# A fused attention and gated-convolution kernel: another order of its hand-written instruction list

## The chip, the core and the metric

The kernel runs on one core of a Trainium2 chip. A core has TensorE (matrix products, written PE in the profile, its weight loads PEld), VectorE (DVE), ScalarE (ACT), GpSimd (POOL) and SyncE (SP), which each work through a list of their own in order and wait for one another by semaphores, and 16 DMA engines that all lists share. The metric is device time in microseconds (us). Four runs of the kernel before took 222.66 to 223.70 us, median 223.43.

## What is computed

Eight batches of 576 positions, eight heads of 64. First linear attention with cosine-weighted features, then a gate with a circular convolution and an output product:

```
r   = max(x, 0);  phi(x) = [r * cos_w, r * sin_w]        # q and k
kv  = phi(k)^T v;  z = sum of phi(k);  x = phi(q) kv / (phi(q) z + 1e-6)
x1, x2, x3 = split(x @ w_proj)
x2_conv = irfft(rfft(x2) * rfft(filter))                 # over the 576 positions
out = (x1 * x2_conv * x3) @ w_out
```

## The kernel before

The work is cut into steps, each a Python generator: one `next` on it issues a few instructions and stops. A plan, a string written into the kernel (lines 905 to 987), names the steps in the order in which their pieces are issued, 1139 pieces in all; `run` (line 890) reads it. As every engine works through what it was given in the order of the plan, this string is the order of all five lists. A word is a step with its indices, the first of them the batch; `*3` takes three pieces; after an apostrophe stands the engine where there is a choice (`'v` VectorE; for `pk` and `pq`, `'a` ScalarE). Without it an eviction goes to ScalarE (`ev`, line 131), a `pk` or `pq` piece to VectorE. A leading `~` makes a load wait (`hold`, line 148) for the last VectorE instruction and the last DMA transpose before it in the plan.

Per batch b the steps are:

- loads `Lq`, `Lk`, `Lv` (line 167, issued by GpSimd, converting to 16 bit; six buffers `raw`, so those of batch b-2 are overwritten); for batch 0's first half `Sk`, `Sv` (SyncE). `Lw`, `Lf`, `Lo` load weights and the filter. `pad` clears the unused rows of a buffer.
- `pk` (line 505, ten pieces), `pq` (519, six pieces, the first over 2560 columns, the others over 512), `va` (539): features of k and q, and v, made on ScalarE or VectorE.
- `kv` (556), `qt` (573: transposes of q's features, on TensorE for batches 0 and 1, by DMA later), `num` (600: product, then three VectorE pieces that divide and write `att`).
- `fx` (629) and `xp` or `xt` (666, 659): `att` into the order that the transform wants, and transposed.
- `pr` (676), `dft` (701), `mul` (718, four VectorE pieces), `inv` (765): the projection of x2 and its convolution in frequency space.
- `ga`, `gb` (730): the two gate projections; `g` (751) their product; `y` (786, six VectorE pieces); `out` (837: product, eviction, store); `end` (863): the last batch's output tile by tile.
- Set-up tables made from index patterns: `io` (GpSimd), `cols`, `rows`, `tf`, `ti`, `th`, `h`, `feo`; `warm` is twelve products on zeros at the start.

Every TensorE step takes one of four PSUM units (line 70), which is free again when its eviction is done; output tiles go through three buffers `os` (846, 872) and one small one (854). So the place of an eviction in ScalarE's or VectorE's list says when TensorE may go on. Steps of several batches are interleaved: while one batch is in its gates, the next is in its attention.

Of the kernel before, what the change touches and what calls it, by code (L numbers as in the profile page):

```python
# [17 lines left out]
def kernel(  # L18
# [48 lines left out]
    late = {}  # L67
# [822 lines left out]
    def run(plan, **batch):  # L890
# [12 lines left out]
    manual = tc.manual_schedule()  # L903
    manual.__enter__()
    run("""
        cols io0 pad1 Sk0.0 pad2 cols io2 rows io1 cols rows th tf warm0.12 cols*5 Sv0.0
        rows pad0 th'v rows*3 th'v cols*3 rows pk0.0'a*2 rows pk0.0'a*2 tf pk0.0 rows
        pk0.0'a tf pk0.0 cols*2 rows va0.1 cols ones0 rows*2 pk0.0*2 rows va0.0'v pk0.0'a
        th'v Lq0.0 Lq0.1 kv0.0 rows pq0.0 pq0.0'a*4 pq0.0 pq0.1*2 qt0.1 pq0.1*3 Lk0.1 qt0.0
        pq0.1'a qt0.2 kv0.0 qt0.1'b num0.1 tf pk0.1'a pk0.1*3 tf pk0.1 qt0.0'c num0.0 pk0.1  # L910
        ones1 pk0.1'a pk0.1*2 Lv0.1 va0.2 num0.0 num0.1 pk0.1'a va0.3'v qt0.2'b Lw0 kv0.1*2
        num0.1 num0.0 num0.1 cols Lw2 num0.0 qt0.3 rows Lq1.2 num0.2*2 cols*2 xp0.0 qt0.3'b
        rows num0.2 rows num0.2 Lk1.2 xp0.0*2 xp0.0'a num0.3*4 xp0.1 Lv1.2 ga0.0 gb0.3 Lw1
        xp0.1*2 pad4 cols pad5 ti xp0.1'v cols pad3 Lf gb0.0*2 tf ga0.0 gb0.0 ga0.0 Lf
        gb0.3*2 ga0.3 gb0.2 ti tf th ~Lq2.2 cols ~Lk2.2 cols pq1.2*2 pq1.2'a pq1.2*2 pq1.2'a
        rows gb0.2 ga0.3 ga0.1*2 ga0.3'v ti cols fx0.1 fx0.0 pk1.2 gb0.2 pk1.2 gb0.1*2 ga0.1
        fx0.3 fx0.1 pk1.2*2 fx0.0'v ga0.2 pk1.2 fx0.2 th gb0.1 fx0.3 fx0.2 ga0.2*2 pk1.2
        tf'v pk1.2*4 qt1.0 va1.0'v kv1.2 va1.1'v kv1.2 th kv1.2 qt1.1 g0.0.2 qt1.0'v th
        ~Lq3.1 tf qt1.0'v qt1.1'v qt1.2 qt1.1'v qt1.2 ~Lk3.0 qt1.2 num1.0*3 tf pr0.1 th
        num1.1 num1.0 num1.2 g0.2.2 num1.1 tf ~Lq3.0 num1.2 num1.1 pr0.1 tf ti pr0.0 num1.2  # L920
        num1.1 qt1.3 num1.2 pr0.0 pr0.2 qt1.3 dft0.0 feo0 pr0.2 dft0.0 feo1 h0 qt1.3'v xp1.0
        ti xp1.0 pq2.2 fx1.1 pq2.2 h0'v h1 ~Lv2.2 pq2.2 xp1.0 pq2.2 pk2.2 xp1.0'v pk2.2
        pk2.2'a h0 fx1.1 pk2.2 num1.3*3 pq2.2 num1.3 pq2.2 qt2.3 h2 qt2.0 fx1.2 h1 pk2.2 h1
        pk2.2 xp1.1 fx1.3 xp1.1 ~Lk3.1 ~Lq4.1 ~Lv3.1 h2 fx1.2 xp1.1'v fx1.3 xp1.1'v fx1.0
        pk2.2*2 dft0.1 dft0.1'v ~Lo dft0.2 ga1.0 fx1.0 dft0.2 mul0 ti mul0 pr1.0 pr1.2 ti*2
        mul0 ga1.0 mul0 pr1.1 pr1.1'v pr1.0 ga1.0 inv0.1 inv0.0 ~Lq4.0 ti pk2.2 late pr1.2
        dft1.2 dft1.0 dft1.2'v inv0.1 dft1.1 pk2.2 inv0.0 inv0.2 va2.0'v dft1.0 kv2.2 pq3.2
        va2.1'v inv0.3 kv2.2 y0.0.2 ~Lk4.1 y0.0.2 dft1.1 inv0.2 ga1.2*2 mul1 gb1.2 mul1
        qt2.1 kv2.2 num2.0 ~Lv3.0 qt2.2 num2.0 inv0.3 num2.1 pq3.2'a ga1.2 gb1.2 ~Lv4.0
        num2.1 num2.0 num2.1 num2.0 num2.1 gb1.3*2 mul1*2 gb1.2 gb1.1*2 pq3.2'a pq3.2 gb1.3  # L930
        pq3.2'a ga1.1 pk3.2 gb1.1 num2.2 ~Lk4.0 num2.2*3 y0.0.2 ga1.1 y0.0.2 fx2.1 y0.2.2
        ga1.1 y0.2.2 gb1.0*2 pk3.2'a fx2.1 inv1.1 fx2.2 pk3.2 gb1.0 inv1.1 fx2.2 ga1.3
        y0.2.2 ga1.3 inv1.0 inv1.0'v ga1.3 xp2.0 num2.3*3 xp2.0*3 num2.3 pk3.2 inv1.3*2
        y0.0.2 inv1.2*2 fx2.0*2 fx2.3*2 g1.0.2 ga2.0 xp2.1*2 pr2.0 xp2.1*2 pq3.2 ga2.0
        y0.2.2 qt3.0 va3.0'v y1.0.2 pk3.2 pk3.2'a*2 pk3.2 y0.2.2 pk3.2'a pq4.2 pr2.1 ga2.0
        qt3.2 pq4.2 out0.0 pr2.2 pr2.1 pr2.0 out0.0 dft2.1 y1.0.2 dft2.0 ~Lq5.0 va3.1'v
        y1.0.2 ~Lq5.1 ~Lv4.1 y1.0.2 pk3.2 ~Lv5.0 qt3.1 y1.2.2*2 pr2.2'v dft2.1 y1.2.2 dft2.2
        kv3.2*2 y1.0.2 gb2.1 y0.2.2 gb2.1 dft2.0 g1.2.2 y0.0.2 pq4.2'a ~Lv5.1 qt3.3 dft2.2'v
        kv3.2 gb2.0*2 mul2*2 num3.0*4 ~Lk5.0 gb2.1 gb2.0 gb2.3 pk4.2'a gb2.3*2 ~Lk5.1 out0.2
        ga2.2*2 fx3.0 out0.2 pq4.2'a ga2.1 mul2*2 ga2.2 fx3.0 num3.1*2 num3.2*2 pk4.2'a  # L940
        ga2.1 num3.1 pk4.2 out0.1 num3.2 num3.1 y1.2.2 ga2.1 num3.2 num3.3*2 pk4.2 pk4.2'a
        num3.3*2 ga2.3 gb2.2 ga2.3 xt3 pq4.2'a gb2.2 out0.1 fx3.1 fx3.2 ga2.3 inv2.1 gb2.2
        fx3.3 pq4.2 qt4.0 qt4.1 pk4.2'a pk4.2*2 fx3.3 fx3.1'v fx3.2'v inv2.1 pk4.2'a inv2.0
        pk4.2 inv2.0 g2.2.2 qt4.2 va4.0'v va4.1'v y2.0.2*2 pr3.0*2 pr3.1 pq5.2 pr3.1 kv4.2
        g2.0.2 y1.2.2 ~Lk6.0 ~Lq6.0 kv4.2*2 pq5.2'a pr3.2 ga3.0 pk5.2 pr3.2'v pk5.2 y1.2.2
        ga3.0 inv2.2 out0.2 dft3.2 ~Lk6.1 inv2.2'v dft3.0*2 dft3.2'v dft3.1*2 num4.0 inv2.3
        pk5.2*2 inv2.3 num4.0 y1.0.2 pq5.2'a gb3.1 num4.1 num4.0*2 num4.2 mul3 gb3.1 num4.1
        ~Lq6.1 pq5.2'a out1.0*2 num4.2 num4.1 pq5.2'a qt4.3 num4.1 ga3.1*2 pq5.2'a y2.0.2
        num4.2 gb3.0 num4.2 y2.0.2 y2.2.2 num4.3 gb3.0 num4.3 out0.0 out1.1*2 y2.2.2 num4.3
        gb3.3 fx4.0 qt5.2 num4.3 fx4.2 gb3.2 mul3 xt4 gb3.3'v ga3.2 qt5.1 mul3 pk5.2 fx4.0  # L950
        fx4.2 mul3 fx4.1 g3.0.2 inv3.0 qt5.0 gb3.2 qt5.3 fx4.3 y2.2.2 ga3.2 fx4.1 pk5.2*3
        inv3.0'v fx4.3 pk5.2 inv3.1 inv3.1'v y2.2.2 y3.0.2*2 pk5.2'a pr4.0 y3.0.2 inv3.3
        pr4.0 y2.2.2 inv3.3 out1.2*2 pr4.2 out1.2 pr4.1 y3.0.2 ~Lq7.0 va5.0'v kv5.2 y2.0.2
        va5.1'v pr4.1'v inv3.2 pq6.2 pr4.2 kv5.2 ga4.0 pk6.2*2 ~Lv6.1 ga4.0'v inv3.2 kv5.2
        out0.1 dft4.2 pq6.2 pq6.2'a*2 pq6.2 dft4.1 dft4.0 ga3.3 dft4.2 dft4.0'v pk6.2 dft4.1
        mul4 ~Lq7.1 num5.0*3 ga3.3 ~Lv6.0 num5.0 ~Lk7.1 gb4.1 num5.1*2 g3.2.2 pk6.2'a*2
        out2.0 gb4.1 y3.2.2 out1.0 out2.0 pk6.2'a pk6.2 pk6.2'a gb4.0 num5.1 gb4.0 num5.1
        out2.1 mul4 num5.2 ~Lk7.0 ga4.1 ga4.2 out2.1 fx5.1 num5.2 y2.2.2 num5.2*2 num5.3*4
        ga4.1 ga4.2 fx5.0 fx5.1 fx5.2 fx5.0 y2.0.2 gb4.2 gb4.2'v mul4 fx5.3 fx5.2 out2.2
        fx5.3 va6.0 pq6.2'a g4.0.2 pr5.2 pr5.2'v pk6.2'a pr5.0*2 out2.2 y3.2.2*2 pr5.1 mul4  # L960
        pk6.2'a va6.1'v pr5.1'v inv4.1*2 y3.2.2 inv4.0 inv4.3 dft5.1 xt5 inv4.0 inv4.3 qt6.0
        dft5.2 pq7.2 dft5.0 ga5.0 dft5.1 dft5.2'v pq7.2*2 y3.2.2 y4.0.2 y3.2.2 dft5.0 out1.1
# [24 lines left out]
    """)
    manual.__exit__(None, None, None)

# [29 lines left out]
```

## Time and profile before

| | |
|---|---|
| median of 4 runs | 223.43 us (222.66 to 223.70) |
| profiled execution: its time, its span | 223.55 us, 221.7 us |
| gate products (line 736), TensorE | 512 matmuls, 71.2 us, mean 286 ns |
| projection of x2 (680) | 160 matmuls, 34.6 us, mean 381 ns |
| output product (824) | 128 matmuls, 30.1 us, mean 379 ns |
| `att` products (116), VectorE | 32, 26.0 us, mean 820 ns |
| evictions of 576 columns: ScalarE, VectorE | about 0.64 us, about 0.75 us |
| HBM read, written | 33.69 MB, 9.44 MB; 194 GB/s over the span |

The profiled execution is one of the runs. Durations in it overlap: an instruction is counted from its start to its end, and the next one on the same engine often starts some 0.1 us earlier than that end. In a group's line stand the source line, engine, operation, result and operands, the count, the busy time, the mean in ns, and the idle time ahead of it with what ended it. In the chain of waits the columns are start, duration and what ran. The view by stretch gives busy time and number of instructions for TensorE, its weight loads, VectorE, ScalarE and GpSimd, then the clock granted to TensorE, the DMA share and GB/s. Lines 111, 116 and 138 are helpers that many steps use, so names of results tell the step.

### The profile page before, as it was taken

Reading aid. Unit: us, or ns where it says so; the run is one execution under the profiler, and the core shown is the slowest. Engines: PE = TensorE matmul, PEld = TensorE weight load, DVE = VectorE, ACT = ScalarE, POOL = GpSimd, SP = SyncE. Lnnn points to the kernel's source line nnn. Section 1 sums busy time; section 2 is a strip of 40 time slices with the busy share of each in tenths; the row PEclk is TensorE's granted clock in tenths of the full one; section 3 lists DMA queues with packets and bytes.
Section 4 is the critical chain, followed back from the end, with each engine's and each line's share of the span. In section 5 each row is a group of like instructions: output and inputs, shape, how many; then the busy total and the mean of one; then the engine's idle time right before and its main releaser. Section 6 shows DMA issues by size and latency. Waiting matters only on the chain.

```text
span 221.7 us, 5869 instructions
## 1 busy us (share of the span) xinstructions
PE 207.8 (94%) x2316; PEld 143.5 (65%) x2316; DVE 195.0 (88%) x473; ACT 170.8 (77%) x275; POOL 63.5 (29%) x105
## 2 busy tenths in 40 slices
PE   7398989999999999999999999999999999999990
PEld 2286777574788567766685768576876667477630
DVE  7898999999999989998999997999988897689930
ACT  4795998998988999878876787977887736476651
POOL 8892425221963077202700184002200000000000
PEclk9859999999999999999999999999999999999999
DMA  5999999999999999999999999997999950823084
GB/s 174 180 188 192 192 209 192 181 116 198 152 177 189 173 168 183 167 204 153 186 163 229 208 185 182 201 250 154 110 188 141 327 134 9 199 95 135 19 260 166
DMA packets 90907, 38.39 MB, mean 173 GB/s; under 512 B 58944, under 2 KB 86592, under 8 KB 90880
## 3 DMA queue, kind: packets, MB, share of 16 engines
q0 software_dynamic: 38944, 16.26, 60.5%
q1 hardware_dynamic: 51568, 21.17, 45.6%
q10 hardware_dynamic: 368, 0.59, 0.7%
q8 instruction: 18, 0.29, 0.5%
q14 instruction: 9, 0.07, 0.1%
HBM read 33.69 MB, written 9.44 MB: 194 GB/s over the span
## 4 chain that ended last, share of the span: by engine, by line
PE 71%; DVE 14%; DMA 5%; ACT 3%; issue 2%; POOL 2%; ACTq 0%; DVEq 0%; POOLq 0%
PE x L736 22%; PE x L680 13%; PE out L824 10%; PE dft L711 4%; PE kv L563 4%; PE num L606 4%; PE fx L634 3%; PE inv L770 3%; PE inv L774 3%; DMA out_dram<-os 3%; DMA raw<-in_q_dram 3%; DVE kp L111 2%; DVE yf L116 2%; DVE qp L111 2%; PE fx L640 1%
## 5 line engine op out<-in xcount | busy, mean ns | idle before, releaser
L736 PE MATMUL x<-xt,wp 128*128 128x288 f16 x512 | 71.2, 286 | 0.3 <-ACT xt L138 0.2
L736 PEld LDWEIGHTS <-wp 128*128 128x128 f16 x512 | 47.9, 98 | 15.4 <-issue 3.2
L680 PE MATMUL x<-wp,fx 128*128 128x512 f16 (+1 forms) x160 | 34.6, 381 | 0.0
L824 PE MATMUL out<-wo,y 128*128 128x512 f16 x128 | 30.1, 379 | 0.0
L138 ACT ACTIVATE os<-out 128x1024 f32<-128x1024 f32 (+2 forms) x24 | 18.3, 767 | 12.0 <-PE out L824 11.8
L116 DVE TENSOR_TENSOR att<-num,rcp 128x640 f16<-128x640 f32 x32 | 26.0, 820 | 0.6
L680 PEld LDWEIGHTS <-fx 128*128 128x128 f16 (+1 forms) x160 | 13.6, 100 | 15.0 <-issue 2.1
L138 ACT CAST x0s<-x 128x576 f16<-128x576 f32 x27 | 17.3, 643 | 6.1 <-PE x L736 5.6
L138 ACT CAST x2s<-x 128x576 f16<-128x576 f32 x28 | 17.8, 639 | 4.8 <-PE x L736 4.7
L138 ACT ACTIVATE x2f<-x 128x1024 f16<-128x1024 f32 (+1 forms) x18 | 16.2, 903 | 6.6 <-PE x L680 5.6
L158 POOL DMA_DIRECT2D raw<-in_q_dram x14 | 11.2, 797 | 32.0 <-ACT xf L138 17.4
L824 PEld LDWEIGHTS <-y 128*128 128x128 f16 x128 | 12.1, 98 | 12.6 <-issue 0.4
L138 ACT CAST fx<-fx 128x576 f16<-128x576 f32 x29 | 17.8, 649 | 2.1 <-PE fx L640 1.8
L138 ACT CAST eq<-inv 128x576 f16<-128x576 f32 x26 | 16.0, 648 | 3.8 <-PE inv L774 3.0
L158 POOL DMA_DIRECT2D raw<-in_k_dram x13 | 10.1, 778 | 27.3 <-DVE ye L116 13.9
L563 PE MATMUL kv<-va,kp 128*128 128x65 f16 x320 | 12.9, 197 | 4.6 <-DVE va L134 4.6
L770 PE MATMUL inv<-itab,yf 128*128 128x144 f16 x128 | 16.9, 226 | 0.2 <-DVE yf L116 0.2
L774 PE MATMUL inv<-itl,yf 128*128 128x288 f16 x64 | 16.8, 286 | 0.0
L158 POOL DMA_DIRECT2D raw<-in_v_dram x13 | 10.5, 806 | 21.7 <-DVE rcp L116 16.9
L563 PEld LDWEIGHTS <-kp 128*128 128x128 f16 x320 | 12.1, 100 | 6.1 <-ACT kp L514 4.0
L606 PEld LDWEIGHTS <-qpt 128*128 128x128 f16 x320 | 13.5, 100 | 3.4 <-issue 0.9
L606 PE MATMUL num<-kvs,qpt 128*128 128x65 f16 x320 | 14.8, 197 | 0.7 <-ACT qpt L138 0.5
(163 smaller groups left out, 431.1 us busy)
## 6 DMA issues: line engine op xcount, KB each, us to landing
out_dram<-os SPq DMA_DIRECT2D x30, 256.0 KB, 3.1
raw<-in_q_dram POOLq DMA_DIRECT2D x12, 256.0 KB, 7.1
raw<-in_k_dram POOLq DMA_DIRECT2D x11, 256.0 KB, 6.6
raw<-in_v_dram POOLq DMA_DIRECT2D x11, 256.0 KB, 6.7
wp<-in_moe_w_proj_dram POOLq DMA_DIRECT2D x3, 512.0 KB, 9.1
raw<-in_q_dram POOLq DMA_DIRECT2D x2, 512.0 KB, 11.8
raw<-in_k_dram POOLq DMA_DIRECT2D x2, 512.0 KB, 13.2
raw<-in_v_dram POOLq DMA_DIRECT2D x2, 512.0 KB, 10.4
```

The source lines that it names most:

```text
L111: last_dve[0] = nc.vector.tensor_scalar(out=out, in0=in0, scalar1=s1, scalar2=s2, op0=op0, **({"op1": op1} if op1 else {}))
L116: last_dve[0] = nc.vector.tensor_tensor(out=out, in0=in0, in1=in1, op=op)
L138: return nc.scalar.copy(out=out, in_=in_) if mul is None else nc.scalar.mul(out=out, in_=in_, mul=mul)
L158: first = queue.dma_start(out=rw[:, to, 0 : 4 * D], in_=src[b, hs, 0:NM].rearrange("h (p j) d -> p h (j d)", j=4),)
L563: nc.tensor.matmul(u[:, g, ds((h % 4) * 65, 65)], kp[:, j, h].rearrange("p a b -> p (a b)"), va[:, h, j, 0:65], start=(j == 0), stop=(j == ...
L606: nc.tensor.matmul(u[:, hh, ds(t * 65, 65)], qpt_buf[:, h, ds(t * 128, 128)], kvs[:, h // 4, ds((h % 4) * 65, 65)], start=True, stop=True,)
L680: nc.tensor.matmul(dst, fx[:, c, ds(128 * ch, n)], wp16[:, c, ds(DM, DM)], start=(c == cs[0]), stop=(c == cs[-1]),)
L711: nc.tensor.matmul(u[ds(32 * x, 32), comp, 0:n], st, mv, start=True, stop=True)
L736: nc.tensor.matmul(u[:, hf, 0:HS], wp16[:, i, ds(w * DM + c * 128, 128)], xt[:, i, ds(HS * hf, HS)], start=(i == 0), stop=(i == NC - 1),)
L770: nc.tensor.matmul(u[:, comp, ds(par * QS, QS)], yf[:, comp, ds(par * DM + c * 128, 128)], itab[:, par + 4 * comp], start=(par == 0), stop ...
L774: nc.tensor.matmul(u[:, comp, 0:HS], yf[:, comp, 2 * DM : NF], itl[:, c, comp].rearrange("p a b -> p (a b)"), start=False, stop=True,)
L824: nc.tensor.matmul(dst, y[:, c, ds(QS * t, 128)], wo16[:, c], start=(c == 0), stop=(c == NC - 1),)
```

## The change

The string is replaced by another one. Both have the same 1139 pieces with the same instructions; what differs is the order of the pieces, and for 115 of them the engine (`'v` and `'a`). The rest of the kernel is unchanged. Its beginning, the places in batches 3 to 6 that the text below speaks of, and the end:

```diff
--- before.py
+++ after.py
@@ -903,87 +903,89 @@
     manual = tc.manual_schedule()
     manual.__enter__()
     run("""
-        cols io0 pad1 Sk0.0 pad2 cols io2 rows io1 cols rows th tf warm0.12 cols*5 Sv0.0
-        rows pad0 th'v rows*3 th'v cols*3 rows pk0.0'a*2 rows pk0.0'a*2 tf pk0.0 rows
-        pk0.0'a tf pk0.0 cols*2 rows va0.1 cols ones0 rows*2 pk0.0*2 rows va0.0'v pk0.0'a
-        th'v Lq0.0 Lq0.1 kv0.0 rows pq0.0 pq0.0'a*4 pq0.0 pq0.1*2 qt0.1 pq0.1*3 Lk0.1 qt0.0
-        pq0.1'a qt0.2 kv0.0 qt0.1'b num0.1 tf pk0.1'a pk0.1*3 tf pk0.1 qt0.0'c num0.0 pk0.1
-        ones1 pk0.1'a pk0.1*2 Lv0.1 va0.2 num0.0 num0.1 pk0.1'a va0.3'v qt0.2'b Lw0 kv0.1*2
-        num0.1 num0.0 num0.1 cols Lw2 num0.0 qt0.3 rows Lq1.2 num0.2*2 cols*2 xp0.0 qt0.3'b
-        rows num0.2 rows num0.2 Lk1.2 xp0.0*2 xp0.0'a num0.3*4 xp0.1 Lv1.2 ga0.0 gb0.3 Lw1
-        xp0.1*2 pad4 cols pad5 ti xp0.1'v cols pad3 Lf gb0.0*2 tf ga0.0 gb0.0 ga0.0 Lf
-        gb0.3*2 ga0.3 gb0.2 ti tf th ~Lq2.2 cols ~Lk2.2 cols pq1.2*2 pq1.2'a pq1.2*2 pq1.2'a
-        rows gb0.2 ga0.3 ga0.1*2 ga0.3'v ti cols fx0.1 fx0.0 pk1.2 gb0.2 pk1.2 gb0.1*2 ga0.1
-        fx0.3 fx0.1 pk1.2*2 fx0.0'v ga0.2 pk1.2 fx0.2 th gb0.1 fx0.3 fx0.2 ga0.2*2 pk1.2
-        tf'v pk1.2*4 qt1.0 va1.0'v kv1.2 va1.1'v kv1.2 th kv1.2 qt1.1 g0.0.2 qt1.0'v th
-        ...
-        pk4.2 inv2.0 g2.2.2 qt4.2 va4.0'v va4.1'v y2.0.2*2 pr3.0*2 pr3.1 pq5.2 pr3.1 kv4.2
-        g2.0.2 y1.2.2 ~Lk6.0 ~Lq6.0 kv4.2*2 pq5.2'a pr3.2 ga3.0 pk5.2 pr3.2'v pk5.2 y1.2.2
-        ...
-        inv7.1 inv7.3 y6.2.2 inv7.2 ga7.3 y6.2.2 y7.0.2*2 inv7.3 gb7.3 y7.0.2*2 out6.0
-        inv7.2 y7.0.2 y7.2.1 out5.0 y7.2.1 y7.3.1*2 y7.2.1*2 ga7.3 out6.0 out6.1 y6.0.2
-        y7.2.1 gb7.3 out6.2 out5.2 out6.1 y7.3.1*2 g7.3.1 y7.3.1 end0*2 end3 end0 out6.0
-        end2 out6.1 out6.2 end1 y7.2.1 end1*3 end2 y7.0.2 end4 y7.3.1 end4 end0 end2 end3*3
-        out6.2 end2 end4'v end4
+        pad2 Sk0.0 io1 pad3 cols io2 th rows io0 th'v pad1 warm0.12 cols*3 th'v rows*4 cols
+        tf pad4 pk0.0'a*2 cols Sv0.0 cols pk0.0'a cols pk0.0'a pk0.0 rows pk0.0'a cols
+        rows*2 pk0.0*2 th'v rows pk0.0'a rows*3 va0.0 rows cols ones0 cols rows*2 cols*2 tf
+        pk0.0 tf pad0 va0.1 tf kv0.0 Lq0.0 pq0.0 tf cols pq0.0'a*4 Lq0.1 kv0.0'v pq0.0'a
+        qt0.1 pq0.1*4 pq0.1'a*2 qt0.1'b qt0.0 qt0.2 num0.1 Lk0.1 pk0.1 pk0.1'a pk0.1 Lv0.1
+        va0.2 pk0.1*3 qt0.0'c pk0.1*2 pk0.1'a num0.0 va0.3'v pk0.1 num0.0 kv0.1 num0.1
+        qt0.2'b qt0.3 num0.1 Lw0 kv0.1 num0.0 num0.1 num0.2 num0.0 num0.2 xp0.0*2 qt0.3'b
+        xp0.0 Lw2 rows*2 num0.2 rows num0.3 num0.2 tf num0.3 xp0.0'a cols*2 xp0.1 ga0.0 cols
+        num0.3*2 gb0.0 tf xp0.1 gb0.2 cols*2 xp0.1 xp0.1'v Lq1.2 ti tf'v cols ga0.0*2 pad5
+        gb0.2*2 ti ones1 th tf gb0.0 Lk1.2 gb0.0 cols ti Lv1.2 pq1.2*2 cols th pq1.2 Lw1
+        pq1.2*2 Lf fx0.0 Lf gb0.3*2 fx0.0'v ga0.1 ~Lq2.2 ga0.1 ga0.3*2 gb0.3 fx0.1 ~Lk2.2
+        gb0.1 ga0.1 pk1.2*2 pk1.2'a ga0.3'v pk1.2*3 pk1.2'a fx0.1 gb0.1 pk1.2 gb0.1 fx0.3
+        pk1.2 pq1.2 pk1.2 fx0.3 ga0.2*2 ~Lq3.0 th va1.0'v qt1.0 qt1.0'v ga0.2 fx0.2 qt1.0
+        va1.1'v fx0.2'v kv1.2*2 g0.2.2 qt1.1 qt1.1'v*2 kv1.2 th qt1.2 num1.0 tf qt1.2'v
+        ...
+        y1.2.2*2 inv2.0 pk4.2 pr3.1 va4.1'v pk4.2 y1.2.2 inv2.1 y1.2.2*2 pr3.0 va4.0'v
+        inv2.0'v pr3.2 pq5.2'a g2.0.2 y2.0.2 kv4.2 pr3.1 y2.0.2 kv4.2 y2.0.2 xt3 inv2.2
+        kv4.2 pr3.2 qt4.1 pk5.2 inv2.2 qt4.0 ga3.0*2 qt4.2 g2.2.2 dft3.2 va5.1'v dft3.0
+        ...
+        out1.1 mul3*2 y1.2.2 mul3 out1.1 fx4.0*2 fx4.1 pq6.2 fx4.1 gb3.3 fx4.3*2 qt5.2 ga3.2
+        ...
+        inv7.1 y7.0.2*2 y6.2.2 inv7.2 out5.2 out5.2'v inv7.3 out6.0 ga7.3 out5.2 inv7.3
+        y7.0.2*2 y7.3.1 y7.2.1 out6.0 y7.0.2 out6.0 out6.1 y7.2.1 y7.3.1 y7.2.1*2 y7.3.1
+        y7.2.1 end0 y7.3.1 ga7.3 out6.2 g7.3.1 y7.3.1 out6.1*2 end0 end0'v end1 end3
+        out6.2'v y7.3.1 y7.0.2 end1 end1'v y7.2.1 end2 end4 end2 end2'v end4 end1 end3 end0
+        out6.2 end3 end4'v end3 end2 end4
     """)
     manual.__exit__(None, None, None)
```

## The prediction

> **What bounds the kernel now.** I read the page's engine table first, then TensorE's own waits, then the busy time by stretch, then the chain of waits, then single landings of loads. The table and TensorE's waits:
>
> ```profile
> PE 207.8 (94%) x2316; PEld 143.5 (65%) x2316; DVE 195.0 (88%) x473; ACT 170.8 (77%) x275; POOL 63.5 (29%) x105
> ```
> ```profile
> PE kv L563 <- DVE va L134: 4.6, 3, 3.6
> PE warm L553 <- DVE half_pi L244: 1.2, 1, 1.2
> PE qt L586 <- DVE coef L284: 0.6, 1, 0.6
> PE num L606 <- ACT qpt L138: 0.5, 1, 0.5
> ```
> TensorE hardly waits, and for attention inputs only. By stretch (sums over each stretch, clock granted near the end of the line):
>
> ```profile
> 8.00:16.00 8.00, 6.18 (x77) 5.70 (x76) 7.26 (x33) 7.20 (x14) 7.07 (x10) 0.57 1.39 178
> 16.00:24.00 8.00, 6.37 (x88) 4.83 (x88) 6.92 (x25) 5.48 (x12) 2.12 (x4) 1.00 1.42 194
> 24.00:32.00 8.00, 7.67 (x79) 6.35 (x77) 8.00 (x26) 8.00 (x15) 3.46 (x5) 1.00 1.43 200
> ...
> 120.00:140.00 20.00, 20.00 (x231) 13.75 (x231) 18.53 (x37) 15.27 (x25) 8.21 (x12) 1.00 1.26 193
> ```
> From 72 to 209 us TensorE has no gap; before 72 it has some. Up to 72 VectorE is the full engine (8.00 of 8.00). I also laid the start-to-start time of each matmul kind (0.123 us for the 288-column one, 0.216 for 512 columns) against TensorE's timeline: start minus work done so far is 10.9 us at 22.7, 13.9 at 72 and 15.4 at the last matmul (215.9). So 3 us are lost between 22.7 and 72 and almost nothing later. The chain of waits shows who causes it:
>
> ```profile
> 5.31 5.91 DMA raw<-in_q_dram
> 11.32 1.96 DVE qp L111 x5
> ...
> 16.02 0.49 DVE va L134
> 16.73 0.86 DVE att L116 x2
> 17.61 0.75 PE qt L586 x10
> 18.38 1.24 ACT qpt L138
> ...
> 22.01 0.65 ACT xt L138
> 22.68 0.46 DVE xt L134
> ...
> 31.98 0.41 DVE va L134
> 32.44 1.45 PE kv L563 x40
> ...
> 213.30 3.49 DMA out_dram<-os
> 216.87 0.61 ACT os L138
> 217.48 0.42 DVE os L111
> ```
> One serial thread: the second query load, batch 0's attention, its transposes, then VectorE without a gap to batch 1's `kv` at 32.44. The tail is set by output buffers: the eviction at 216.87 waits for a store begun at 213.30.
>
> **The Trainium skill.** "Perfetto Trace Analysis", Identifying the Most-Contended Engine, says that matmul busy time doesn't show how close TensorE is to its limit; hence my reckoning by start-to-start times, which agrees that 72 to 209 is full. "TensorE: Matmul & The Clock Gate", Part 1, says that an idle TensorE falls to half clock and needs some 3.4 us of activity to recover; the trace agrees (0.57 granted in 8 to 16, after a gap of 3.58). The change keeps that gap, so I cost it at nothing. "DMA: Bandwidth & Descriptors", Issuing engines are not separate DMA queues, says that loads and stores from all engines share 16 DMA engines; here they are 90% busy up to about 180 us, so a load moved in the list can delay another.
>
> **The change, part by part.** No instruction is added or taken away; 115 evictions and activations change between ScalarE and VectorE (net three more on VectorE), and the order of all lists moves by 11 places on average. "List sum" below means: start-to-start times (an eviction of 576 columns 0.53 on ScalarE, 0.68 on VectorE) added along a list.
>
> (1) First 10 us. `pad3`, `pad4` (0.27 each) come early on VectorE, `io0` comes last of the three on GpSimd. ScalarE needs nothing before k32 lands at 4.7, so both are covered. `va0.0` goes to ScalarE: v lands at 8.2, two casts at 0.63 to 0.72 end at 9.6, the last `pk0.0` on VectorE at about 9.8, so `kv0.0` starts at 9.9 against 9.72: cost 0.2, not on the chain.
>
> (2) The query part. ScalarE now does seven `pq` pieces instead of five (0.45 each): its `qt0.1` eviction starts at 12.6 instead of 12.27. It then waits anyway, as before, for v's half at 14.44 (issued at 7.45 to 8.19, 6.2 to 6.7 us), and has one `pk0.1` less before it. Cost nothing. VectorE has 1.0 us more to do before `pq0.1`: 0.7 of it fills the gap before 11.32, the rest costs 0.3; it has 0.4 less between there and `num0.0`, so it is level at 15.8.
>
> (3) `kv0.1` and `qt0.3`. `va0.3` and the last `pk0.1` stand ahead of the two `num` evictions. `va0.3` ran at 15.94 to 16.51; now about 15.1 to 15.95 with the last `pk0.1`. `kv0.1` ends at 16.5 instead of 17.04. `qt0.3` began at 17.61, released just after an `att` product; in the new list its PSUM unit can only be the one that `qt0.2`'s eviction frees (15.48 + 1.21 = 16.69), so it begins near 16.8. Its eviction moves from 18.38 to 17.4, and the sine of `coef` no longer stands ahead of it. Gain 1.0.
>
> (4) To the last transposes. `num0.3` 19.66 to 18.6, its `att` product 20.64 to 19.8, `xp0.1` then 20.6; before the last `xt` copy VectorE still has 1.0 us (`tf`, `fm`, `fme`). It ends at 22.0 instead of 23.14: 1.1 earlier, and by list sum with 0.7 us more work behind it (22.2 against 21.5). TensorE resumes its gates at 22.0 instead of 22.70, having done 12.3 us of its list instead of 11.8: gain 1.2.
>
> (5) To `kv1.2`. VectorE's list sum to the end of `va1.1` is 31.2 after, 30.8 before. From the last `xt` that is 9.0 after, 9.3 before (23.14 + 9.3 = 32.4, as seen). After: 31.0. Loads could spoil it: k of batch 1 lands at 13.20 + 13.1 = 26.3 (its tail at 26.8), v at 14.75 + 14.7 = 29.5 (tail 29.9); I need them at 26.7 and 29.7. Cost 0.1 to 0.2: `kv1.2` at 31.1 instead of 32.44, gain 1.3.
>
> (6) To 72 us. Both lists ask about the same of VectorE up to `num2.3` (67.3 after, 67.6 before), which was busy for 47.1 of the 48 us from 24 to 72. It can be 1.8 to 2.2 ahead; TensorE is 1.3 ahead and can win back part of the 1.5 it lost between 33 and 72. Loads: `Lq2.2` is held 1.0 us longer, `Lq3` and `Lv2.2` go out earlier; each has 3 us or more. I take 2.0 ahead at 72.
>
> (7) 72 to 209. TensorE has nothing to gain. ScalarE gets its share earlier: between 73.8 and 119.7 us of TensorE's list it has 40.7 us instead of 33.5, VectorE 41.4 instead of 42.4. Among it is the first `pq5.2` piece, 2560 columns on ScalarE, which the trace doesn't show: twice the 1280-column copy (1.22) is 2.4, against 0.82 on VectorE; bounds 1.8 and 2.6. Behind it wait `pr3.1`, `kv4.2`, `pr3.2`: counted from the end of `pr3.0`, the unit of `pr3.1` is free at 0.92 + 2.4 + 0.92 = 4.2 and asked for at 4.5. It fits by 0.3. `Lq6` lands about 109 to 110 for a `pq6.2` at about 110. I take 0.1 for all this, bounds 0 and 3.6.
>
> (8) Tail. Last matmuls, three store buffers and their order are as before; `end0`, `end1`, `end2` and `out6.2` are evicted by VectorE instead of ScalarE (0.6 for 0.5). The last evictions still wait for the stores of `end0` and `out6.2`: within 0.3 of before, taken 0.
>
> Sum: -2.0 + 0.1 = -1.9. The profiled execution took 223.55 (span 221.7, 1.85 around it); less 1.9 that is 221.65. The median of the runs (223.43) lies 0.12 lower; I say 221.6.
>
> **The rivals.** *More than that (B)*: all 3 us of gaps between 22.7 and 72 go as well as 0.4 more: 3.4 less, 220.1. For it: VectorE's lead is larger than TensorE's. Against it: several of these gaps are TensorE waiting for VectorE within one batch, which shift with it. *No change (C)*: the lead is real at 22 but loads at 26.8, 29.9 and w1 at 17.74 + 14.6 = 32.3 pace what follows, or it is lost in small gaps later: 223.3. For it: those loads land within 0.3 us of my need. Against it: VectorE, not a load, ended every wait of the chain after 11.32. *Slower (D)*: ScalarE becomes the bound in batches 3 to 5. It was idle for 10.1 us between 88 and 136, largely while waiting for TensorE's results, which it can't fill at will. If half of the 7.2 us that it gets more finds no such place, PSUM units come free late and TensorE loses 3.6: +1.7, 225.1. It decides from 1.9 us lost, about a quarter of the 7.2. Against it: the lists put these pieces where ScalarE waits, as the 0.3 above shows.
>
> **How the numbers follow.** Forecast 0.46, B 0.13, C 0.14, D 0.27. The forecast alone spans 220.7 to 222.7 (steps 3 to 6 by half a us each way, step 8 by 0.3). Eight in ten: 219.9 to 225.1, which leaves out parts of B and D. About 0.3% (0.67 us) is what can be told from no change: faster is the forecast and B, 0.59; same is C, 0.14; slower is D, 0.27.
>
> **What would show it.** `qt0.3` before 17.2, the last `xt` copy before 22.4, `kv1.2` at 31 to 31.5, `num2.3`'s product near 69 instead of 71; then TensorE at 20.00 of 20.00 up to some 207; ScalarE above 17 of 20 between 100 and 140. I am wrong if `kv1.2` isn't earlier (then steps 3 and 4), or if it is and TensorE shows waits for ScalarE between 85 and 135 (then step 7).

## The result, and the profile after

| | before | changed |
|---|---|---|
| median (range) | 223.35 us (221.99 to 225.63), 64 runs | 222.61 us (222.19 to 226.23), 43 runs |
| ratio, 95% interval | | 0.9966 (0.9955 to 0.9977) |
| profiled execution: time, span | 223.55, 221.7 us | 222.98, 221.2 us |

The change gains 0.75 us, 0.34%. The forecast was 1.8. Ratios leave out runs more than 1.5% above the fastest run of the same kernel (six of sixteen in the first experiment below, whose other ten have a median of 225.18 us); medians and ranges are of all runs. The medians hide what turns out to matter most: how far the single runs lie apart. Of the changed kernel's runs eight in ten lie between 222.37 and 222.97; of the 64 runs of the kernel before, between 222.59 and 224.46, and of its 228 runs that went along with the experiments, between 222.78 and 224.63 (worked out from the lists of single runs). The shortest runs are alike, 222.19 and 221.99.

The page's engine table of the changed kernel, and TensorE's longest waits in it (engine, line, what ended the wait: sum, times, longest):

```profile
PE 207.7 (94%) x2316; PEld 143.0 (65%) x2316; DVE 197.9 (89%) x476; ACT 171.9 (78%) x272; POOL 63.1 (29%) x105
```
```profile
PE kv L563 <- DVE va L239: 3.0, 1, 3.0
...
PE kv L563 <- DVE kp L111: 0.7, 1, 0.7
PE x L736 <- ACT x2s L138: 0.4, 1, 0.4
```

Busy time by stretch, of the changed kernel and then, for the two stretches not shown above, of the kernel before:

```profile
8.00:16.00 8.00, 5.81 (x74) 5.42 (x74) 7.70 (x39) 7.12 (x14) 7.03 (x9) 0.57 1.41 184
16.00:24.00 8.00, 7.24 (x97) 5.77 (x98) 7.19 (x27) 6.29 (x14) 1.83 (x3) 1.00 1.45 196
24.00:32.00 8.00, 7.61 (x90) 6.25 (x88) 8.00 (x24) 8.00 (x14) 4.24 (x6) 1.00 1.40 202
56.00:64.00 8.00, 7.49 (x119) 6.17 (x116) 7.71 (x17) 6.91 (x12) 6.81 (x10) 1.00 1.36 143
64.00:72.00 8.00, 7.71 (x95) 6.67 (x95) 6.92 (x16) 6.78 (x13) 5.34 (x8) 1.00 1.50 194
120.00:140.00 20.00, 20.00 (x241) 14.02 (x239) 18.36 (x43) 14.33 (x23) 8.20 (x12) 1.00 1.29 196
```
```profile
56.00:64.00 8.00, 7.87 (x121) 6.36 (x121) 7.97 (x17) 7.22 (x13) 6.41 (x10) 1.00 1.30 150
64.00:72.00 8.00, 7.75 (x104) 6.68 (x103) 7.76 (x20) 7.04 (x13) 4.19 (x7) 1.00 1.49 192
```

The new start is in the second line: TensorE is busy for 7.24 us between 16 and 24 instead of 6.37. From 56 to 72 the changed kernel is the worse one: VectorE works 14.63 us of 16 there instead of 15.73, so it is idle for 1.1 us more. The chain of waits of the changed kernel at its start (start, duration, what):

```profile
11.40 0.31 issue
11.71 1.07 DVE qp L111 x4
12.78 1.15 DVE kp L111 x5
...
16.31 1.56 DVE att L116 x2
17.92 0.75 PE xp L670 x10
...
31.34 0.64 DVE va L134
32.02 0.80 PE kv L563 x20
```

The query load, 5.91 us of the chain before, is not in it. `kv1.2`, in two halves here, is done with the second, and evicted at 33.45 instead of 34.51: 1.06 earlier. The tail is of the same kind as before:

```profile
214.06 2.80 DMA out_dram<-os
216.99 0.42 DVE os L111
```

Followed from landmark to landmark, the lead of these two profiled executions is 1.06 us at 33, 1.07 at 54, 0.35 at 71 and 0.4 to 0.5 at the end. So on first reading the changed kernel makes its lead where it was forecast, and loses two thirds of it between 54 and 71. There ScalarE waits for a load (start, duration, engine, line, operation; in brackets the idle time before it and what ended it):

```profile
62.65 0.72 ACT L514 ACTIVATE kp<-raw,ccol 128x512 f16<-128x512 f16 x1 [0.92 <-DMA raw<-in_k_dram]
63.28 0.62 ACT L138 CAST x2s<-x 128x576 f16<-128x576 f32 x1
```

The load is `Lk3.0`, issued at 56.3 us instead of 35.7. Behind it the gate eviction `x2s` is late, and TensorE waits for that (0.4 us in its waits above; 0.6 counted by start-to-start times).

### The profile page after: what moved, and what is told of

Read it like the earlier page. It is cut to its first block, busy times and chain, and to the rows that moved or that the text cites. A ratio compares the mean times of both kernels' runs of the same rounds, so it can differ in the third digit from the quotient of the medians.

```text
span 221.2 us, 5868 instructions
## 1 busy us (share of the span) xinstructions
PE 207.7 (94%) x2316; PEld 143.0 (65%) x2316; DVE 197.9 (89%) x476; ACT 171.9 (78%) x272; POOL 63.1 (29%) x105
## 4 chain that ended last, share of the span: by engine, by line
PE 71%; DVE 18%; DMA 4%; issue 3%; ACT 2%; POOL 1%; DVEq 0%; SPq 0%; POOLq 0%; ACTq 0%
PE x L736 23%; PE x L680 13%; PE out L824 11%; DVE kp L111 4%; PE kv L563 3%; PE num L606 3%; PE inv L770 3%; PE inv L774 3%; PE dft L711 3%; DMA raw<-in_k_dram 3%; PE fx L634 3%; DVE qp L111 2%; DVE att L116 2%; PE out L829 2%; PE fx L640 1%
## 5 line engine op out<-in xcount | busy, mean ns | idle before, releaser
L138 ACT ACTIVATE x2f<-x 128x1024 f16<-128x1024 f32 (+1 forms) x22 | 19.4, 896 | 7.4 <-PE x L680 7.2
L138 ACT ACTIVATE os<-out 128x1024 f32<-128x1024 f32 (+2 forms) x17 | 13.8, 813 | 12.5 <-DMA out_dram<-os 6.3
L138 ACT CAST x2s<-x 128x576 f16<-128x576 f32 x27 | 17.3, 645 | 3.7 <-PE x L736 2.9
L774 PE MATMUL inv<-itl,yf 128*128 128x288 f16 x64 | 16.8, 286 | 0.0
L138 ACT CAST xf<-dft 128x1024 f16<-128x1024 f32 (+1 forms) x18 | 14.9, 879 | 1.8 <-PE dft L711 1.5
L138 ACT CAST eq<-inv 128x576 f16<-128x576 f32 x23 | 14.3, 650 | 2.2 <-PE inv L774 1.2
L563 PEld LDWEIGHTS <-kp 128*128 128x128 f16 x320 | 11.5, 99 | 6.3 <-ACT va L138 3.5
L116 DVE TENSOR_TENSOR eo<-eq 128x576 f16<-128x576 f16 (+1 forms) x34 | 13.9, 432 | 1.4 <-ACT eq L138 0.9
## 6 DMA issues: line engine op xcount, KB each, us to landing
raw<-in_v_dram POOLq DMA_DIRECT2D x2, 512.0 KB, 10.6
```

Source lines behind the costliest of these rows:

```text
L116: last_dve[0] = nc.vector.tensor_tensor(out=out, in0=in0, in1=in1, op=op)
L138: return nc.scalar.copy(out=out, in_=in_) if mul is None else nc.scalar.mul(out=out, in_=in_, mul=mul)
L563: nc.tensor.matmul(u[:, g, ds((h % 4) * 65, 65)], kp[:, j, h].rearrange("p a b -> p (a b)"), va[:, h, j, 0:65], start=(j == 0), stop=(j == ...
L774: nc.tensor.matmul(u[:, comp, 0:HS], yf[:, comp, 2 * DM : NF], itl[:, c, comp].rearrange("p a b -> p (a b)"), start=False, stop=True,)
```

## The experiments

Times are set against runs of the kernel before on the same chip.

**Is it that load?** First the load alone, placed earlier in the changed plan:

```diff
-  ... ~Lq3.1 num1.3 pk2.2 num1.3
-  dft0.1 dft0.2 ga1.0 qt2.3 qt2.0 ~Lk3.0 fx1.3 dft0.2 ~Lq4.0 ...
+  ... ~Lq3.1 ~Lk3.0 num1.3 pk2.2 num1.3
+  dft0.1 dft0.2 ga1.0 qt2.3 qt2.0 fx1.3 dft0.2 ~Lq4.0 ...
```

> The changed kernel with one load moved: the first half of k of batch 3 (Lk3.0) stands directly behind Lq3.1 instead of behind dft0.1 and the last transposes of batch 1, so it should be issued near 48 us instead of 56.3 and land near 55 instead of 62.6. Theory T (the late load takes the lead back: ScalarE waits 0.9 us for it, x2s is late, TensorE stops for 0.6): the stop of TensorE at 62.4 to 64.0 goes, 0.5 to 0.9 us faster than the changed kernel, about 221.9. Rival R (the order and the engines of the evictions between 54 and 72 take the lead, the load would only be the last of several): within 0.2 us of the changed kernel, 222.5 to 222.7.

Measured: 226.12 us, ratio 1.0069 (1.0035 to 1.0104): slower than either kernel. Neither theory had this. TensorE's longest wait in it is a new one:

```profile
PE num L606 <- DMA qpt<-qp: 2.5, 1, 2.5
```

The load, now issued at 48.1 us, runs beside the four transposes of batch 2's q, which hold SP for 10.92 us instead of 8.59 in the changed kernel's page (7.64 in the profile of the next experiment); `num2.1` waits for them. The late place, 56.3, had kept the load behind nearly all of them. (The Trainium skill, "DMA: Bandwidth & Descriptors", Issuing engines are not separate DMA queues, says that transfers from all engines interleave on the same 16 DMA engines; the trace agrees, with 2.3 to 3.3 us more for four transposes.)

Then the load left alone, and the piece that waits for it moved back:

```diff
-  ... ga1.1 ~Lk4.1 pq3.2'a ~Lo pk3.2'a num2.1 ga1.1
-  ... num2.3*3 ga1.3 pk3.2 inv1.3 y0.2.2
+  ... ga1.1 ~Lk4.1 pq3.2'a ~Lo num2.1 ga1.1
+  ... num2.3*3 ga1.3 pk3.2'a pk3.2 inv1.3 y0.2.2
```

> The changed kernel with the load left where it is; the one piece of k that reads it first (pk3.2, piece 0, on ScalarE) is moved back behind the evictions of gb1.2, ga1.1, gb1.1, gb1.0, fx2.1, fx2.2 to stand just before piece 1. Theory T: ScalarE no longer waits for the load in front of x2s, the stop of TensorE goes too: 0.4 to 0.8 us faster than the changed kernel, about 222.0. Rival R (order and engines as a whole): within 0.2 us of the changed kernel. If this one gains and the earlier load doesn't, or the other way, then the reading of that wait is wrong.

Measured: 222.78 us, ratio 0.9957 (0.9939 to 0.9975): no different from the changed kernel's 0.9966, as rival R said. In the profile TensorE is busy for 7.89 of 8 us between 56 and 64, so the stop is gone, and the total hasn't moved. The reason came with a later profile of the changed kernel's own order there (g2 below), ScalarE at the same place:

```profile
62.00 0.72 ACT L514 ACTIVATE kp<-raw,ccol 128x512 f16<-128x512 f16 x1
62.62 0.64 ACT L138 CAST x2s<-x 128x576 f16<-128x576 f32 x1
```

No wait: the load had landed. TensorE is busy for 7.99 of 8 us there, and for 8.00 and 7.89 in two repeated profiles. The stop at 62 belonged to one execution, not to the kernel. Theory T fell.

**Which stretch brings the gain?** Hybrids of the two plans: one plan up to a landmark, then what is left in the other's order:

```
pre  = first[: first.index(landmark) + 1]
plan = pre + [piece for piece in second if piece not in pre]
```

> The changed kernel's lists up to the end of batch 1's kv (33 us), then the kernel before's order and engines for all that is left, its early Lk3.0 among it. Theory T: the start is worth the 1.05 us read at kv1.2, and nothing takes it back before 72: 1.0 us faster than before, about 222.4. Rival R2 (a lead of TensorE at 33 can't be carried over 72 in either order, because VectorE's work up to num2.3 sets that point): 0.3 us or less, about 223.1.

> The changed kernel's lists up to num2.3 (71 us), then the kernel before's order and engines for all that is left, its tail too. Theory T with the lead of 0.25 to 0.4 us read at 72: 0.3 us faster than before, about 223.1, the other 0.4 being the changed tail. Rival R3 (the tail and the middle are worth nothing): as fast as the changed kernel, 222.6.

> The kernel before's lists up to num2.3 (71 us), then the changed kernel's order and engines for all that is left, its tail too. New theory V (what follows 72 us is worth more than the start: in part of the executions of the kernel before, output evictions on ScalarE near 130 us wait for stores that stand on SP behind the transposes of batch 4, and TensorE then waits; the changed order has the stores 1.4 us earlier): ratio to before 0.997 to 0.999 in the median, and the times no longer spread over 3 us but over about 1. Rival S (the start is all of the gain): the median of the kernel before, ratio 0.9995 or more, and its spread.

> The changed kernel's start (up to the end of batch 1's kv), the kernel before's order from there to num2.3, and the changed kernel's order for the rest. If the start's 0.75 us is carried through the middle of the kernel before, as the trace of the first hybrid shows, and the changed rest keeps it in all executions: 0.3 us faster than the changed kernel, 222.3, ratio to before 0.995. If what the changed middle loses (0.3 to 0.5 us) is of no effect because later waits take it up again: 222.6, as the changed kernel, ratio 0.9965.

> The kernel before's lists up to the end of batch 1's kv (33 us), then the changed kernel's order for all that is left. Theory V: most of the median's gain is in the rest, so 0.998 to 0.9985 of before with a narrow spread, and 0.3 to 0.5 us slower than the changed kernel. Rival S (the start is the gain, and the changed middle loses): as slow as before or 0.3 us slower, ratio 1.000 to 1.001.

| plan to 33 us | 33 to 71 | after 71 | median, runs | ratio to before, 95% |
|---|---|---|---|---|
| changed | changed | changed | 222.61, 43 | 0.9966 (0.9955 to 0.9977) |
| changed | before | before | 223.32, 22 | 0.9989 (0.9968 to 1.0011) |
| changed | changed | before | 223.63, 22 | 0.9996 (0.9972 to 1.0020) |
| before | before | changed | 223.25, 14 | 0.9992 (0.9971 to 1.0012) |
| changed | before | changed | 223.08, 22 | 0.9978 (0.9960 to 0.9995) |
| before | changed | changed | 224.38, 22 | 1.0032 (1.0014 to 1.0049) |

No part alone gives the gain. The changed start in front of the old order is worth most likely 0.25 us, and its interval includes no gain at all; 1.0 was expected (rival R2's 0.3 or less came). The changed order without its own start is slower than before, and the changed start and end around the old middle keep two thirds of the gain: for these two no forecast came. That the parts are fitted to each other is a reading of the table; which pieces must meet isn't shown. In the one profile of the last hybrid 1.1 us is lost after 71, with gate products that wait 0.93 us at 169.6 for batch 6's transpose: the changed order too can be held up by a transfer.

The spread follows the part after 71 more than the median does: eight in ten runs lie within 1.2 to 1.4 us in the three hybrids that have it from the changed kernel, within 1.8 to 1.9 in the two that have it from the kernel before. The changed kernel's own 0.6 needs all three parts.

In the profile of the first hybrid the lead over the profiled execution of the kernel before is about 0.8 us from 33 us to the end, although its median is hardly lower: a sign that this one execution was not a fair yardstick.

**How far apart are executions of one kernel?** The kernel before was profiled three times more and the changed kernel twice, with no edit:

> The kernel before, profiled once more, to see which of its landmarks move from one execution to the next. Theory V: up to 72 us within 0.3 us of the first profile; if this execution is a slow one, what is lost is lost after 100 us at an output eviction. Rival Y (the start varies, with the landing of the second query load): the difference is there by 18 us and constant after it.

> As the one before, for a second time: theory V and rival Y as there.

> The kernel before, profiled a fourth time. Theory Z: num0.1 ends anywhere from 16.5 to 17.6, following the landing of the second query load; after 72 us either nothing is lost against the fastest profile or 0.4 to 1.9 us, at an engine that waits for a load or a store to land. Rival G: within 0.3 us of the first profile at every landmark.

> The changed kernel, profiled once more. Theory Z (the change makes the time depend less on when loads land, in an undisturbed execution both kernels are alike): the first batch's product num0.1 ends at 17.1 to 17.6 whenever the second query load lands, batch 1's kv is evicted at 33.4 to 33.8, and less than 0.3 us is lost after 72 us. The stop of TensorE for x2s near 62 us is not in every execution. Rival G (the gain is a shorter path that every execution has): num2.3's product ends 0.7 us or more before all executions of the kernel before.

> As the one before, for a second time: theory Z and rival G as there.

Landmarks in us (ends of instructions; "first att" is `num0.1`'s product; the means take in every profile with the same list up to that point):

| execution | its time | 2nd query load lands | first att | kv1.2 evicted | num2.3's att | last eviction |
|---|---|---|---|---|---|---|
| before (the page) | 223.55 | 11.2 | 17.56 | 34.51 | 71.15 | 217.91 |
| before, again 1 | 222.69 | 10.8 | 16.54 | 33.64 | 70.31 | 217.08 |
| before, again 2 | 223.95 | 10.9 | 16.98 | 33.82 | 70.72 | 218.34 |
| before, again 3 | 222.79 | 11.0 | 17.02 | 33.87 | 70.43 | 217.18 |
| changed (the page) | 222.98 | 10.7 | 17.13 | 33.45 | 70.80 | 217.42 |
| changed, again 1 | 223.62 | 11.3 | 18.10 | 34.41 | 71.15 | 218.10 |
| changed, again 2 | 223.13 | 10.9 | 17.36 | 33.68 | 70.45 | 217.65 |
| mean, list of before | | | 17.11 (of 10) | 34.05 (of 10) | 70.72 (of 9) | |
| mean, changed list | | | 17.46 (of 10) | 33.76 (of 10) | 70.66 (of 6) | |

Rival Y holds for the first repetition: it is 1.0 us ahead of the page at the first att and 0.8 to 0.9 at every landmark after it. Theory V's "within 0.3 us" up to 72 fails in all three.

The page that the prediction was made from shows the latest `kv1.2` of ten executions with that start. The next three fences show where part of this comes from, one line each from VectorE's timeline: the first piece of the second query half in the page of the kernel before, in its repetition 1, and in the page of the changed kernel.

```profile
11.32 0.65 DVE L111 TENSOR_SCALAR qp<-raw 128x1280 f16<-128x1280 f16 x1 [0.71 <-DMA raw<-in_q_dram]
```
```profile
10.93 0.49 DVE L111 TENSOR_SCALAR qp<-raw 128x1280 f16<-128x1280 f16 x1
```
```profile
11.71 0.48 DVE L111 TENSOR_SCALAR qp<-raw 128x1280 f16<-128x1280 f16 x1
```

With the list of before VectorE gets there between 10.6 and 11.0, and in six of ten profiles it then waits for the load, 0.3 to 0.8 us. The first att then ends anywhere from 16.54 to 17.59; this landing alone doesn't set it (11.2 goes with 17.56, but 11.5 once with 17.19). With the changed list VectorE has other work until 11.55 to 11.83, and the load has landed by then in all ten: later on average, less exposed. Batch 1's `kv` is evicted at 33.45 to 33.85 in nine of ten (34.41 in the other, where this piece took 0.92 us instead of 0.48), against 33.64 to 34.51. The mean lead is 0.3 us there and 0.1 at 71. Rival G, a shorter path in every execution, is out; theory Z holds in kind, but not in its numbers: one of the two repetitions misses its windows for the first att (18.10) and for `kv1.2` (34.41), and from 71 on they take 0.3 and 0.6 us more than the page (146.96 and 147.19 against 146.62).

One thing stays unexplained. The three profiled executions of the changed kernel took 222.98, 223.62 and 223.13, all in the upper tenth of its 43 runs, while those of the kernel before lie on both sides of its median. The two repetitions ran on a chip from which the record has no other runs of the changed kernel, so the chip may be a reason. Either way the traces don't show the typical changed execution, and the 0.75 us can't be divided up from them to the last tenth.

**Where does the kernel before lose in its longer executions?** From `num2.3`'s att to the last eviction three of its four profiles take 146.75 to 146.77 us, the fourth takes 147.62, 0.9 more. The profile of the second hybrid has the same order there and loses 1.8 us between 108 and 137. An output eviction at 111.50 us waits 1.40 us for a store; most is lost in these lines (ScalarE's timeline, then TensorE's waits):

```profile
130.32 1.03 ACT L138 ACTIVATE os<-out 128x1024 f32<-128x1024 f32 x1 [1.46 <-DMA out_dram<-os]
...
134.86 1.02 ACT L138 ACTIVATE os<-out 128x1024 f32<-128x1024 f32 x1 [1.77 <-DMA out_dram<-os]
```
```profile
PE fx L634 <- ACT os L138: 1.2, 1, 1.2
```

Output evictions wait for stores to leave their buffer. SP's timeline of repetition 1 of the kernel before (nothing lost), and of this hybrid:

```profile
111.87 5.92 SPq L660 DMA_TRANSPOSE xt<-att  x1
117.83 4.57 SPq L577 DMA_TRANSPOSE qpt<-qp  x3
...
124.41 2.06 SPq L850 DMA_DIRECT2D out_dram<-os  x4
```
```profile
112.36 7.36 SPq L660 DMA_TRANSPOSE xt<-att  x1
119.76 5.40 SPq L577 DMA_TRANSPOSE qpt<-qp  x3
...
126.48 2.08 SPq L850 DMA_DIRECT2D out_dram<-os  x4
```

The stores (line 850) stand behind batch 4's transpose `xt4` (line 660), and that takes 5.9 us or 7.4. Hence four edits:

```diff
 # f4, kernel before: the two stores ahead of the q transposes
-  ... mul3 xt4 gb3.3'v ga3.2 qt5.1 mul3 pk5.2 fx4.0
+  ... mul3 xt4 gb3.3'v ga3.2 out0.1 out1.0 qt5.1 mul3 pk5.2 fx4.0
 # g1, g2, both kernels: stores of batches 0 to 5 write 64 of 512 columns
+        w = 64 if b < 6 else DM
-            nc.sync.dma_start(out=out_rows(b, tiles[i]), in_=os_[:, i])
+            nc.sync.dma_start(out=out_rows(b, tiles[i])[:, 0:w], in_=os_[:, i, 0:w])
 # k1, kernel before
-  fx5.3 va6.0 pq6.2'a
+  fx5.3 va6.0'v pq6.2'a
```

> The kernel before with one thing moved: the stores of two finished output tiles (out0.1, evicted near 86 us, and out1.0, evicted at 107) stand on SP directly behind the transposes xt4, ahead of qt5.1, qt5.0 and qt5.3, instead of behind them: near 118.5 to 120.5 instead of 125 to 127. Theory V: the evictions of out2.0 and out2.1 never wait, the spread of 3 us shrinks to about 1, the median is 0.3 to 0.6 us lower (ratio 0.9975 to 0.9985). Rival W (the spread comes from transposes and loads whose length varies, the stores only follow them): median and spread of before; if the transposes of q of batch 5, now 2 us later, are late for num5: 0.3 us or more slower.

Measured: 225.83 us, ratio 1.0106 (1.0065 to 1.0146). The price was the one named last, and larger: the q transposes behind the stores, issued at 122.4 instead of 117.8 to 119.8 and 6.06 us long, hold up batch 5's attention:

```profile
PE num L606 <- DMA qpt<-qp: 2.1, 1, 2.1
```

> The kernel before, its stores of the output tiles of batches 0 to 5 cut to 64 of 512 columns (most of the output is left unwritten; everything else as it was). Theory V (in its slower executions the kernel before loses at evictions that wait for stores to land): the spread shrinks from 3 us to about 1, the median falls by 0.5 to 0.9, to 222.7. Rival X (the slower executions come from loads or transposes that take longer, stores only among them): the median falls by 0.3 or less and the spread stays 2 us or more.

> The changed kernel with the same cut stores. Theory V: it had no such waits, so it stays within 0.2 us of the changed kernel (ratio to before 0.996 to 0.997), and stands level with the kernel before with cut stores, within 0.3. Rival X: it falls as far as that one does, and stays 0.7 us ahead of it.

Measured: 222.89 us, 0.9978 (0.9960 to 0.9996), and 222.88 us, 0.9974 (0.9959 to 0.9989). These two kernels leave most of the output unwritten. With short stores they are equal in the median, within their intervals, and the changed one hasn't gained. That is theory V's forecast for the pair; the spread of the first shrinks only in part, to 222.48 to 223.65 for eight in ten runs. So what the changed kernel has over the other in the median goes when the stores are short. The store's traffic also gets smaller, so this shows that stores take part, not that the buffers alone do.

> The kernel before with one cast moved, as the change has it: v of batch 6, first half of the list (va6.0), on VectorE instead of ScalarE, where in one profile it waited 1.1 us for its load with the evictions of pr5.2 to inv4.1 queued behind it. Theory Z: that wait no longer holds evictions up, the slowest executions become rarer: 0.1 to 0.4 us lower in the median, ratio 0.998 to 0.9995. Rival N (that wait was a symptom, the same landing is waited for elsewhere): ratio 0.9995 to 1.001, the spread as before.

Measured: 223.49 us, 0.9998 (0.9969 to 1.0028): rival N. Its profile is one more with the waits for stores (1.39, 1.41 and 1.85 us) and `xt4` at 7.86.

Over all profiles `xt4` holds SP for 7.2 to 7.9 us in four of nine with the old order there, and those four have evictions that wait for stores (at 111.5 to 111.9 us in all four, near 130 only in the second hybrid and k1, not in all four as the expectation for m1 has it); it takes 4.3 to 5.6 in all nine with the new order. In the old order `qt5.2` stands directly ahead of it, in the new one behind. The last two edits swap just these:

```diff
 # m1, kernel before
-  gb3.3 fx4.0 qt5.2 num4.3 fx4.2 gb3.2 mul3 xt4 gb3.3'v ga3.2
+  gb3.3 fx4.0 num4.3 fx4.2 gb3.2 mul3 xt4 qt5.2 gb3.3'v ga3.2
 # m2, changed kernel
-  num4.3 xt4 pk5.2 ... fx4.3*2 qt5.2 ga3.2
+  num4.3 pk5.2 ... fx4.3*2 qt5.2 xt4 ga3.2
```

> The kernel before with one transpose moved on SP: that of q of batch 5 for one pair of heads (qt5.2), which stood directly ahead of the transpose of batch 4's att (xt4), stands directly behind it, as the change has it. In the profiles so far xt4 holds SP for 4.8 to 5.9 us or for 7.2 to 7.9 behind qt5.2 (nine profiles, four of them over 7, and just those four have evictions that wait for stores near 130 us), and for 4.3 to 5.6 where it comes first (nine profiles). Theory M (the pair of transposes and the loads beside them make the slow executions): xt4 stays under 5.7 us, no eviction waits for a store near 130, the median falls by 0.3 to 0.5 us (ratio 0.998 to 0.9987) and the upper tenth from 224.6 to below 223.8. Rival L (the four loads issued from 103.7 instead of 104.5 make it, whatever the order on SP): xt4 over 7 us in part of the executions still, median and spread of before, ratio 0.9995 or more.

> The changed kernel with the opposite edit: xt4 directly behind qt5.2 instead of ahead of it. Theory M: the slow executions come back, the upper tenth goes from 222.97 to 224 or more, the median to 222.9 to 223.3 (ratio 0.998 to 0.9995). Rival L: as the changed kernel, 222.6 and a spread under 1 us, ratio 0.9966.

Measured: m1 223.64 us, 1.0004 (0.9985 to 1.0023), no gain, its eight in ten from 222.99 to 224.40. m2 222.66 us, 0.9964 (0.9945 to 0.9984), the median of the changed kernel; its upper tenth begins at 223.36 instead of 222.97, and its profiled execution (224.12) has `xt4` at 6.50 us and a wait that the profiles of the changed kernel don't have:

```profile
PE x L736 <- DMA xt<-att: 0.9, 1, 0.9
```

So the swap may give the changed kernel some longer executions (e2 and g2, without it, have their upper tenth from 223.19 and 223.45), and the opposite swap doesn't cure the kernel before. Theory M fell as the one cause; both results lie where rival L put them.

The same traces hold a difference ahead of `xt4` that no experiment went after. It lies in two output stores on SP and the first of the four loads on GpSimd; first repetition 1 of the kernel before, then the second hybrid:

```profile
103.06 1.18 SPq L850 DMA_DIRECT2D out_dram<-os  x2
103.69 0.75 POOL L158 DMA_DIRECT2D raw<-in_k_dram  x1 [14.01 <-DVE rcp L617]
```
```profile
104.13 1.16 SPq L850 DMA_DIRECT2D out_dram<-os  x2
104.15 0.75 POOL L158 DMA_DIRECT2D raw<-in_k_dram  x1 [13.20 <-ACT xf L138]
```

In four profiles (repetitions 1 and 3, the first hybrid, m1) the stores go out 0.6 us ahead of the load. The second store then lands 4.4 to 4.8 us after its issue, `xt4` takes 5.9 to 6.0 us, and from 71 on they take 146.75 to 146.77 us. In five others with full stores and the old order (the page, repetition 2, the second hybrid, k1, f4) stores and load go out within 0.02 us of each other. The second store lands 6.5 to 6.6 us after its issue, and four of the five have the long `xt4` and lose time; the page is the fifth, where the store landed 0.1 us before it was needed. It is this store that the evictions at 111.5 to 111.9 wait for, and they have waited before `xt4` is issued at 112.2 to 112.7. So the long transpose isn't the first delay. With short stores (g1) the pair goes out together too and nothing is lost. In all ten profiles with the changed order the stores lead by 1.2 us or more, and no such eviction waits. Rival L's reason doesn't fit: the executions whose loads go out earliest, at 103.7, lose nothing. That stores and load meet is thus the likelier origin, but it goes along with the loss and no run tests it.

What stays open is what decides whether they meet, and which of the many moves keep them apart. No run here beats the changed kernel: e2 and m2 are level with it, and so are g1 and g2, which write less; everything else is slower.

## Why the prediction was wrong

Steps 1 and 2: the start on VectorE was read as level at 15.8, with "0.7 of it fills the gap before 11.32". That gap was the landing of a load in one execution. On average the changed start is 0.35 us later at the first att product. The step failed as a statement about the kernel, and the next three inherit it.

Steps 3 to 5: right against the one profile, and near in size: `qt0.3` at 16.59 (16.8 forecast), the last `xt` at 22.26 (22.0), TensorE resumes its gates at 21.82 (22.0), `kv1.2` 1.06 us earlier (1.3). Between means of ten it is 0.3. The mechanism shows in the means too: from the first att, where the changed list is 0.35 us behind, to `kv1.2`, where it is 0.3 ahead, it gains 0.64. The size of the lead is off by a factor of four: 0.46 of the missing 1.0 is the base, the latest start of ten, and the rest is the changed list itself, whose mean of 33.76 lies 0.55 behind the 33.2 that the step implies. That the two pages differ by 1.06 was luck, the latest start of one list against the earliest of the other.

Step 6 is the step of the sum that failed: "I take 2.0 ahead at 72". Measured are 0.35 between the two pages and 0.1 between the means. The forecast wanted VectorE's lead to grow and TensorE to win back part of 1.5 us of gaps. TensorE's busy time from 32 to 72 is 38.76 us before and 38.78 after: no gap was won back. And the step's list of loads left out `Lk3.0`, which goes out 20 us later; in one profile it came 0.92 us late. Of the six profiles in the mean at 71 five don't have that wait, and the 0.3 won by `kv1.2` is down to 0.1 all the same; what takes it isn't shown.

Step 7: 0.1 was forecast, and TensorE is busy for all of the 128 us from 72 to 200 in the profile of the changed kernel, with no wait for ScalarE between 85 and 135. ScalarE is busy for 18.64 us of 20 from 100 to 120 as forecast, but for 14.33 from 120 to 140. The unknown piece of 2560 columns on ScalarE, estimated at 2.4 us, from the groups by form:

```profile
L526 ACT ACTIVATE qp<-raw 128x2560 f16<-128x2560 f16 x1 | 2.3, 2328 | 0.0
```

The prediction's own figures, 13.9 at 72 and 15.4 at the last matmul, put 1.5 us of TensorE's losses after 72, where it speaks of almost nothing. What step 7 lacked is the other sign. The kernel before and the hybrids with its order lose 0.9 to 1.9 us after 71 in part of their executions, and the profile that was read happened to be one that doesn't. Some of the 0.75 us is probably won here, and no term of the sum had it: the pair with short stores speaks for it, but the hybrid with only this part changed (0.9992, 0.9971 to 1.0012) doesn't show it.

Step 8 held: the last eviction lies 0.5 us earlier with a lead of 0.4.

The rivals: B and D didn't come. C, "lost in small gaps later", is what the traces show up to 71 us. The direction came true by luck: the 2.0 us that was to carry it didn't come, and most of the gain probably lies outside the sum.

## What to carry to other kernels

One profiled execution is a sample: before pricing a change of one or two us, profile the same kernel three or four times and take each landmark's mean, and look above all at loads whose landing ends a wait. In this case the changed order has a shorter start by 0.3 us on average and fewer waits for landings; much of its gain is in the spread of the runs, and no single trace has that. Single moves in such an order (a load 8 us earlier, two stores 5 us earlier) cost 2 us or more against the kernel they were made in, each time because transposes beside or behind them came late for a product.

## What the runs showed of the hardware

A transpose by DMA varies by microseconds from one execution to the next: the same `xt4` held SP for 5.6 to 7.9 us in the old order with full stores. The four loads issued just ahead of it took from 6.1 to 10.8 us to land there, and 5.6 to 7.1 in three profiles of the changed kernel.

TensorE's stop of 2.5 us in the first experiment was followed by 3.4 us at half clock (0.61 and 0.54 granted from 64 to 68), and the kernel ended 3.8 us behind. The stop of 2.1 us in f4 left the clock at 1.00. "TensorE: Matmul & The Clock Gate", Part 1, of the Trainium skill gives some 3.4 us of idleness as the measure, in a window that runs freely; here 2.5 was enough once.
